# Weight words of the block sums from DRAM, and a scaling behind a maximum on GpSimd

## The chip, the cores and the metric

The kernel runs on 1 core of one Trainium2 chip. The metric is the device time of one execution in microseconds (us). Five engines of the core work beside each other, each through its own instructions in order: PE (TensorE, matrix products), DVE (VectorE), ACT (ScalarE), POOL (GpSimd) and SP (SyncE, which here only issues transfers). An instruction starts when its operands are there and its engine has reached it. Transfers (DMA) run on 16 DMA engines that all queues share.

## The reference

The program is an attention over narrow windows, followed by a feed-forward layer.

```python
B, H, S, D = 8, 8, 576, 64
scores = (q @ k.T) / sqrt(D)                # heads 0-3: the last 32 positions
scores = where(mask, scores, -1e9)          # heads 4-7: every 4th of the last 128
attn = exp(scores - max(scores)); attn = attn / (sum(attn) + 1e-9)
x = (attn @ v).transpose(0, 2, 1, 3).reshape(4608, 512)
h = x @ w_in                                # 512 x 2048, float32
g = h * clip(h + 3, 0, 6) / 6
out = g @ w_out                             # 2048 x 512, float32
```

The weights arrive as 64-bit words. Each float32 operand of the feed-forward products is split into a high and a low part, and three products of parts stand for one product, so the precision of float32 is kept.

## The kernel before, in words

**Weights.** The two weight matrices come in 32 half blocks p of 512 KB (`st`, issued by SP at L484; even p for w_in, odd p for w_out). A half block goes through a chain of seven instructions: ACT takes two scaled copies (U, L499, and Q, L503), DVE shifts (s, L507), sets the sign (j, L513) and adds (a, `cv_add`, L520); what stands in `va` then is the rounded float32 word. ACT copies its high part (h, L523) and DVE subtracts it to get the low part (l, L529), both into the long-lived tiles `wi` or `wo`.

**The first part of the program** (the last addition L520 starts at 151.5 us) is a hand-written order, one string of names, with these seven letters in it for each p. It holds the first attention tiles, all conversions, and the first products of chunk 0 and 1. What comes behind it is a list of operations that a planner sorts: every operation has an engine, an assumed duration, operations it comes after, and slots that it takes and gives back.

**Chunks and groups.** The 4608 tokens make twelve chunks of 384. The first four are plain: first product L545 to L547, gate, second product L595 to L597. The gate's high part `gh` is a CAST on POOL (L560) for these. The other eight chunks go through the products of blocks in seven instead of eight multiplications (L754 to L756 for the first, L745 for the second weight matrix). Their stationary operands are sums and differences of weight blocks. They lie in two DRAM arrays, `sums` and `rights`, and stream back through a ring of eight tiles of 512 KB (L689), issued by SP.

**The block sums** are made once, in the planned part, for 2 sides x 8 pairs k. For each: two DVE additions of high and low part give the words back (`combo_words`, L640), four DVE instructions make the sums (L648), ACT takes the high parts (L652), DVE the low parts (L657), and SP writes both (L675, two transfers of 512 KB). Three plain blocks of each pair are written from `wi` or `wo` (L666, three transfers of 256 KB). The slots of `wi` and `wo` come free when the additions, the plain writes and the products that use them are done.

**Slots.** All these tiles (st, va, wi, wo, v, sh, ring, out) come from one pool of 36 slots of 4 KB a partition. The next user of a slot waits for the last reader of it, whatever engine or queue that is on.

**Attention in the planned part.** A beat of PE computes scores of one tile (L227) and values of an older one (L245). `kq` and `v` (L195, L204) are loaded by SP. Behind the scores DVE takes the largest of each row (L279), multiplies it by minus the scale (L280, 128x6), and ACT takes exponents with it as bias (L288). POOL moves finished attention rows into chunk tiles (L453, L455).

Of the kernel before, what the change touches and what calls it, by code (L numbers as in the profile page):

```python
# [85 lines left out]
def windowed_attention_ffn(ctx: ExitStack, tc: tile.TileContext, qk, vp, w, mask, out, out_t):  # L86
# [183 lines left out]
            in1=mx.rearrange("p (s o) -> p s o", o=1).broadcast_to([P, SLOTS, 2 * QB]), op=ALU.subtract,  # L270
        )

    def scaled_largest(t):
        ps, masked = pss[t]
        if not masked:
            ps = es[t]
        mx = small.tile([P, SLOTS], F32, name="mx")
        pss[t] = ps, mx, masked
        nc.vector.tensor_reduce(out=mx, in_=ps[:, :CH].rearrange("p (s x) -> p s x", x=2 * QB), axis=AX.X, op=ALU.max)  # L279
        nc.vector.tensor_scalar_mul(mx, mx, -SCALE)  # L280

    def exponents(t, j):
        ps, mx, masked = pss[t]
# [233 lines left out]

    def cv_add(p):
        _, _, v, a = parts(p)
        return nc.vector.tensor_tensor(out=v.bitcast(U32), in0=v.bitcast(U32), in1=a.bitcast(U32), op=ALU.add)  # L520

    def cv_high(p):
        ins = nc.scalar.copy(wt(p // 2, p % 2 * 2), parts(p)[2])  # L523
# [3 lines left out]
    def cv_low(p):  # L527
        hi, lo = (wt(p // 2, p % 2 * 2 + i) for i in range(2))
        freed = nc.vector.tensor_tensor(out=lo, in0=parts(p)[2], in1=hi.bitcast(F32), op=ALU.subtract)  # L529
        last["converted"] = freed.ins.name  # L530
        del staged[p]
        converted.add(p)
        return freed

    phs, ts, ghs, gls, po, done = {}, {}, {}, {}, {}, set()

# [95 lines left out]
    ]  # L632
    KEPT = (T1, T3, T4, T2, R11, R21, R22)

    def combo_words(side, k, i, eng):

        if (side, k) not in combos:
            combos[side, k] = w_tile("v", [4, HALF])
        x, v = (win, wout)[side][2 * k + i], combos[side, k]
        eng.tensor_tensor(  # L640
            out=v[:, 2 * i : 2 * i + 2].rearrange("p a n -> p (a n)"), in0=x[:, 0].bitcast(F32), in1=x[:, 1].bitcast(F32), op=ALU.add
        )

    def combo_sum(side, k, i, eng):

# [175 lines left out]
    def attend(bs, pools):  # L821
# [18 lines left out]
            takes=list(room.items()), gives=[("work", len(values))],  # L840
        )
        for ts in scores:
            if by_tensor(ts):
                x = op("DVE", 0.68, lambda ts=ts: scaled_largest(ts), [beat], ahead=EVER)
            else:
                x = op("DVE", 0.55, lambda ts=ts: add_mask(ts), [beat], takes=ONE, gives=[(names[ts], 1)], ahead=EVER)
                released[names[ts]].append(x)
                x = op("DVE", 0.68, lambda ts=ts: scaled_largest(ts), [x], ahead=EVER)
            for i in range(3):
                holds = not i and by_tensor(ts)  # L850
                x = op(
                    "ACT", 0.54, lambda ts=ts, i=i: exponents(ts, i), [x], takes=ONE if holds else (),
                    gives=[(names[ts], 1)] if i == 2 and by_tensor(ts) else (), ahead=EVER,
                )
            if by_tensor(ts):
                released[names[ts]].append(x)
            turned[ts] = turn_over(ts, es, ats, "a", x)
            if ts + NLOAD < T:
                landed_k[ts + NLOAD] = transfer(0.4, 0.82, lambda ts=ts: load_qk(ts + NLOAD), [beat])
# [44 lines left out]

    gated_h = {}

    words, combined, taken = {}, {}, {}

    def combine(side, k):
        x = op("DVE", 0.69, lambda: combo_words(side, k, 0, nc.vector), takes=[("w", 2, SPARE[side][k])], ahead=LEAD_SUMS)  # L910
        words[side, k] = x = op("DVE", 0.69, lambda: combo_words(side, k, 1, nc.vector), [x], ahead=EVER)
        for i in range(4):
            x = op("DVE", 0.42, lambda i=i: combo_sum(side, k, i, nc.vector), [x], ahead=EVER)
        x = op("ACT", 1.05, lambda: combo_high(side, k), [x], ahead=EVER)
# [6 lines left out]
    def last_use(side, f, x):  # L921

        taken[side, f] = x
        if f % 2:
            k = f // 2
            op("NONE", 0.0, lambda: None, [words[side, k], combined[side, k][1], taken[side, f - 1], x], gives=[("w", 2)], ahead=EVER)

    def first(n, after):
        c, f = steps[n]
# [618 lines left out]
```

## Time and profile before

| | us |
|---|---|
| median of 3 runs | 834.25 |
| lowest and highest run | 833.37, 834.36 |
| span of the profiled execution | 832.4 |
| PE busy | 818.8 (98%) |
| DVE busy | 651.2 (78%) |
| ACT busy | 577.0 (69%) |
| POOL busy | 59.3 (7%) |
| moved by DMA | 214.70 MB, mean 258 GB/s |

The profile shows one execution. A run's time contains its span and what lies around it; the median is 1.85 us longer than this span. The chain of waits goes back from the last instruction to what released it each time. The table of windows gives each engine's busy time in stretches of the span, with the share in which the 16 DMA engines were busy and what they moved. In the timeline of SP a row is a transfer's issue, not its movement.

### The profile page before, as it was taken

To read this page: it belongs to the slowest core of one execution; us is meant where nothing else is said; L and a number is where in the kernel's file an instruction comes from. 1 tells how busy PE (TensorE), PEld (TensorE's weight loads), DVE (VectorE), ACT (ScalarE), POOL (GpSimd) and SP (SyncE) were. 2 spreads that over 40 slices of the span, in tenths; PEclk is the share of its full clock that TensorE was granted. 3 is DMA by queue.
4 is the path that set the end of the run, shared out by engine and by line. 5 is a ranking of instruction groups with operands and counts; after the bars stand their busy time and mean duration, and the time that the engine had idled before them with its cause. 6 is when DMAs were issued, how large, how long until landed. Compare 5 with 4: busy or idle time off the path is not lost.

```text
span 832.4 us, 22160 instructions
## 1 busy us (share of the span) xinstructions
PE 818.8 (98%) x8743; PEld 772.0 (93%) x8743; DVE 651.2 (78%) x1325; ACT 577.0 (69%) x1406; POOL 59.3 (7%) x114
## 2 busy tenths in 40 slices
PE   7899999999999999999999999999999999999998
PEld 4788999898898888999999999999999999999998
DVE  4998997656788989888989786888776888445983
ACT  3878775244899884899965699955698845355552
POOL 0000000011223221001300000100001000000000
PEclk9999999999999999999999999999999999999999
DMA  8756433262679999999986798977788777896381
GB/s 289 245 201 239 127 108 118 78 228 93 214 226 304 295 366 357 352 394 393 380 299 228 270 322 312 344 253 258 261 309 308 248 268 254 314 353 239 114 297 57
DMA packets 115783, 214.70 MB, mean 258 GB/s; under 512 B 7520, under 2 KB 40288, under 8 KB 115680
## 3 DMA queue, kind: packets, MB, share of 16 engines
q1 hardware_dynamic: 115680, 213.29, 73.6%
q8 instruction: 69, 1.13, 0.5%
q14 instruction: 34, 0.28, 0.1%
HBM read 174.47 MB, written 38.80 MB: 256 GB/s over the span
## 4 chain that ended last, share of the span: by engine, by line
PE 94%; DVE 2%; DMA 2%; ACT 1%; issue 1%; SPq 0%
PE ps_o L745 28%; PE ps_x L754 10%; PE ps_x L756 9%; PE ps_x L755 9%; PE ps_o L596 5%; PE ps_o L597 5%; PE ps_o L595 5%; PE ps_h L545 5%; PE ps_h L546 5%; PE ps_h L547 5%; PE ps_b L245 2%; PE ps_b L227 1%; PE ps_a L245 1%; PE ps_a L227 1%; DMA st<-in_w 1%; DMA first<-in_v 1%
## 5 line engine op out<-in xcount | busy, mean ns | idle before, releaser
L745 PE MATMUL ps_o<-gh,ring 128*128 128x384 f32 x896 | 230.2, 334 | 0.0
L745 PEld LDWEIGHTS ps_o<-gh,ring 128*128 128x128 f32 x896 | 162.1, 188 | 0.0
L745 PE MATMUL ps_o<-gl,ring 128*128 128x384 f32 x448 | 149.7, 334 | 0.0
L1208 DVE TENSOR_TENSOR gl<-g,gh 128x384 fp32r<-128x384 f32 x224 | 115.8, 552 | 20.8 <-ACT gh L1204 19.8
L1204 ACT CAST gh<-g 128x384 fp32r<-128x384 f32 x224 | 104.7, 512 | 33.3 <-PE ps_o L745 25.1
L754 PE MATMUL ps_x<-x,ring 128*128 128x384 f32 x256 | 88.4, 345 | 0.0
L545 PE MATMUL ps_h<-x,wi 128*128 128x384 f32 x256 | 87.8, 343 | 0.0
L755 PE MATMUL ps_x<-x,ring 128*128 128x384 f32 x256 | 86.1, 336 | 0.0
L756 PE MATMUL ps_x<-x,ring 128*128 128x384 f32 x256 | 86.1, 336 | 0.0
L546 PE MATMUL ps_h<-x,wi 128*128 128x384 f32 x256 | 86.0, 336 | 0.0
L547 PE MATMUL ps_h<-x,wi 128*128 128x384 f32 x256 | 86.0, 336 | 0.0
L745 PEld LDWEIGHTS ps_o<-gl,ring 128*128 128x128 f32 x448 | 84.1, 188 | 0.0
L596 PE MATMUL ps_o<-wo,gh 128*128 128x512 f32 x192 | 74.8, 390 | 0.2 <-DVE wo L529 0.2
L595 PE MATMUL ps_o<-wo,gh 128*128 128x512 f32 x192 | 74.9, 390 | 0.0
L597 PE MATMUL ps_o<-wo,gl 128*128 128x512 f32 x192 | 74.7, 389 | 0.0
L553 ACT ACTIVATE t<-ps_h,three 128x384 f32<-128x384 f32 x64 | 37.0, 581 | 52.4 <-PE ps_h L547 52.1
L756 PE MATMUL ps_x<-cell,ring 128*128 128x384 f32 x192 | 64.9, 338 | 0.0
L754 PE MATMUL ps_x<-cell,ring 128*128 128x384 f32 x192 | 64.7, 337 | 0.0
L755 PE MATMUL ps_x<-cell,ring 128*128 128x384 f32 x192 | 64.7, 337 | 0.0
L1173 DVE TENSOR_TENSOR g<-g 128x768 f32<-128x768 f32 x64 | 60.9, 952 | 0.0
L556 DVE SCALAR_TENSOR_TENSOR t<-t,ps_h 128x384 f32<-128x384 f32 x64 | 35.0, 549 | 23.1 <-ACT t L553 22.7
L392 ACT COPY xf<-xf_t 32x192 f32<-32x192 f32 x144 | 50.4, 350 | 2.8 <-DVE xf L385 0.4
(113 smaller groups left out, 1744.9 us busy)
## 6 DMA issues: line engine op xcount, KB each, us to landing
ring<-sums SPq DMA_DIRECT2D x112, 512.0 KB, 8.3
ring<-rights SPq DMA_DIRECT2D x112, 512.0 KB, 6.7
st<-in_w SPq DMA_DIRECT2D x32, 512.0 KB, 3.9
kq<-in_qk SPq DMA_DIRECT2D x39, 416.0 KB, 5.2
v<-in_v SPq DMA_DIRECT2D x39, 390.0 KB, 6.6
sums<-wi SPq DMA_DIRECT2D x24, 256.0 KB, 6.9
rights<-wo SPq DMA_DIRECT2D x24, 256.0 KB, 6.1
out<-o SPq DMA_DIRECT2D x15, 384.0 KB, 2.8
```

The lines of the kernel that those rows point to most:

```text
L545: nc.tensor.matmul(ph, lhsT=wt(f, 0)[:, ks], rhs=a, start=(kt == 0), stop=False)
L546: nc.tensor.matmul(ph, lhsT=wt(f, 0)[:, ks], rhs=b, start=False, stop=False)
L547: ins = nc.tensor.matmul(ph, lhsT=wt(f, 1)[:, ks], rhs=a, start=False, stop=(kt == NK - 1))
L595: nc.tensor.matmul(po[c][tt], lhsT=gh[:, rows], rhs=wt(f, 2), start=first, stop=False)
L596: nc.tensor.matmul(po[c][tt], lhsT=gh[:, rows], rhs=wt(f, 3), start=False, stop=False)
L597: return nc.tensor.matmul(po[c][tt], lhsT=gl[:, rows], rhs=wt(f, 2), start=False, stop=(f == NF - 1))
L745: nc.tensor.matmul(banks[part][:, :CH], lhsT=right[:, a, cols], rhs=x, start=(start and not i), stop=(i == 2), skip_group_check=True)
L754: nc.tensor.matmul(bank, lhsT=tile_[:, 0, ks], rhs=h[:, kt], start=(start and kt == 0), stop=False, skip_group_check=True)
L755: nc.tensor.matmul(bank, lhsT=tile_[:, 0, ks], rhs=l[:, kt], start=False, stop=False, skip_group_check=True)
L756: nc.tensor.matmul(bank, lhsT=tile_[:, 1, ks], rhs=h[:, kt], start=False, stop=(kt == 1), skip_group_check=True)
L1204: nc.scalar.copy(two[0], gated_tile(g, q, k))
L1208: nc.vector.tensor_tensor(out=two[1], in0=gated_tile(g, q, k), in1=two[0].bitcast(F32), op=ALU.subtract)
```

## The change

Three things change.

1. **A write at conversion.** `cv_add` also issues a transfer on GpSimd's queue that writes the rounded word of the half block (256 KB, 2 KB a partition row) into a new DRAM array `rounded`. There are 32 of them, 8.4 MB. The slot of `va` is now free only when its write has landed.
2. **A load at the block sum.** The 32 DVE additions of `combo_words` go. In their place SP loads the two half blocks of a pair from `rounded` in one transfer of 512 KB (`combo_load`, L645 of the changed kernel; 16 of them, 8.4 MB). The release of the `wi` and `wo` slots no longer names the words. The planner counts the load with 0.5 us of SP and 1.0 us of transfer.
3. **The small multiplication.** Behind the maximum in the planned part, the multiplication of 128x6 by minus the scale goes from DVE to GpSimd (36 of them, L283 of the changed kernel). The planner counts 0.5 us for the maximum and 0.2 us of POOL for the multiplication, where it counted 0.68 us of DVE for both.

```diff
@@ -270,14 +270,17 @@
             in1=mx.rearrange("p (s o) -> p s o", o=1).broadcast_to([P, SLOTS, 2 * QB]), op=ALU.subtract,
         )
 
-    def scaled_largest(t):
+    def plain_largest(t):
         ps, masked = pss[t]
         if not masked:
             ps = es[t]
         mx = small.tile([P, SLOTS], F32, name="mx")
         pss[t] = ps, mx, masked
         nc.vector.tensor_reduce(out=mx, in_=ps[:, :CH].rearrange("p (s x) -> p s x", x=2 * QB), axis=AX.X, op=ALU.max)
-        nc.vector.tensor_scalar_mul(mx, mx, -SCALE)
+
+    def scaled(t):
+        mx = pss[t][1]
+        nc.gpsimd.tensor_scalar_mul(mx, mx, -SCALE)
 
     def exponents(t, j):
         ps, mx, masked = pss[t]
@@ -517,7 +520,9 @@
 
     def cv_add(p):
         _, _, v, a = parts(p)
-        return nc.vector.tensor_tensor(out=v.bitcast(U32), in0=v.bitcast(U32), in1=a.bitcast(U32), op=ALU.add)
+        ins = nc.vector.tensor_tensor(out=v.bitcast(U32), in0=v.bitcast(U32), in1=a.bitcast(U32), op=ALU.add)
+        nc.gpsimd.dma_start(out=rounded[p % 2, p // 4][:, p // 2 % 2], in_=v)
+        return ins
 
     def cv_high(p):
         ins = nc.scalar.copy(wt(p // 2, p % 2 * 2), parts(p)[2])
@@ -531,6 +536,8 @@
         del staged[p]
         converted.add(p)
         return freed
+
+    rounded = tc.dram_tile([2, NF // 2, P, 2, WN], F32, name="rounded")
 
     phs, ts, ghs, gls, po, done = {}, {}, {}, {}, {}, set()
 
@@ -632,14 +639,10 @@
     ]
     KEPT = (T1, T3, T4, T2, R11, R21, R22)
 
-    def combo_words(side, k, i, eng):
-
-        if (side, k) not in combos:
-            combos[side, k] = w_tile("v", [4, HALF])
-        x, v = (win, wout)[side][2 * k + i], combos[side, k]
-        eng.tensor_tensor(
-            out=v[:, 2 * i : 2 * i + 2].rearrange("p a n -> p (a n)"), in0=x[:, 0].bitcast(F32), in1=x[:, 1].bitcast(F32), op=ALU.add
-        )
+    def combo_load(side, k):
+
+        combos[side, k] = v = w_tile("v", [4, HALF])
+        nc.sync.dma_start(out=v.rearrange("p a n -> p (a n)"), in_=rounded[side, k].rearrange("p i n -> p (i n)"))
 
     def combo_sum(side, k, i, eng):
 
@@ -840,12 +843,12 @@
             takes=list(room.items()), gives=[("work", len(values))],
         )
         for ts in scores:
-            if by_tensor(ts):
-                x = op("DVE", 0.68, lambda ts=ts: scaled_largest(ts), [beat], ahead=EVER)
-            else:
+            x = beat
+            if not by_tensor(ts):
                 x = op("DVE", 0.55, lambda ts=ts: add_mask(ts), [beat], takes=ONE, gives=[(names[ts], 1)], ahead=EVER)
                 released[names[ts]].append(x)
-                x = op("DVE", 0.68, lambda ts=ts: scaled_largest(ts), [x], ahead=EVER)
+            x = op("DVE", 0.5, lambda ts=ts: plain_largest(ts), [x], ahead=EVER)
+            x = op("POOL", 0.2, lambda ts=ts: scaled(ts), [x], ahead=EVER)
             for i in range(3):
                 holds = not i and by_tensor(ts)
                 x = op(
@@ -904,11 +907,10 @@
 
     gated_h = {}
 
-    words, combined, taken = {}, {}, {}
+    combined, taken = {}, {}
 
     def combine(side, k):
-        x = op("DVE", 0.69, lambda: combo_words(side, k, 0, nc.vector), takes=[("w", 2, SPARE[side][k])], ahead=LEAD_SUMS)
-        words[side, k] = x = op("DVE", 0.69, lambda: combo_words(side, k, 1, nc.vector), [x], ahead=EVER)
+        x = transfer(0.5, 1.0, lambda: combo_load(side, k), takes=[("w", 2, SPARE[side][k])], ahead=LEAD_SUMS)
         for i in range(4):
             x = op("DVE", 0.42, lambda i=i: combo_sum(side, k, i, nc.vector), [x], ahead=EVER)
         x = op("ACT", 1.05, lambda: combo_high(side, k), [x], ahead=EVER)
@@ -923,7 +925,7 @@
         taken[side, f] = x
         if f % 2:
             k = f // 2
-            op("NONE", 0.0, lambda: None, [words[side, k], combined[side, k][1], taken[side, f - 1], x], gives=[("w", 2)], ahead=EVER)
+            op("NONE", 0.0, lambda: None, [combined[side, k][1], taken[side, f - 1], x], gives=[("w", 2)], ahead=EVER)
 
     def first(n, after):
         c, f = steps[n]
```

The order of PE's instructions is the same in both kernels. Since the planner sorts again, the others move.

**SP, where the ring begins.** `rights` and `sums` are the DRAM arrays, `wo` the converted weights, `sh` and `v` the block sums' parts, and `v<-rounded` the new load. Before:

```order
L675 DMA sums_107<-sh_4463 128x4x256
L675 DMA sums_107<-v_4129 128x4x256
L666 DMA rights_108<-wo_1895 256x1x256
L666 DMA rights_108<-wo_1963 256x1x256 x2
L689 DMA ring_4672<-sums_107 128x2x512
L666 DMA rights_108<-wo_2065 256x1x256
L666 DMA rights_108<-wo_2160 256x1x256 x2
L666 DMA rights_108<-wo_1522 256x1x256
L666 DMA rights_108<-wo_1502 256x1x256 x2
L689 DMA ring_4734<-sums_107 128x2x512
L689 DMA ring_4773<-sums_107 128x2x512
L689 DMA ring_4820<-sums_107 128x2x512
```

Changed:

```order
L645 DMA v_4664<-rounded_107 128x1024
L645 DMA v_4669<-rounded_107 128x1024
L645 DMA v_4677<-rounded_107 128x1024
L669 DMA rights_109<-wo_1919 256x1x256
L669 DMA rights_109<-wo_1990 256x1x256 x2
L669 DMA rights_109<-wo_2095 256x1x256
L669 DMA rights_109<-wo_2191 256x1x256 x2
L678 DMA sums_108<-sh_4633 128x4x256
L678 DMA sums_108<-v_4056 128x4x256
L669 DMA rights_109<-wo_1535 256x1x256
L669 DMA rights_109<-wo_1515 256x1x256 x2
L692 DMA ring_4787<-sums_108 128x2x512
```

Before, the first ring load stood ahead of six plain writes; now all plain writes and all 16 loads of words, three of them in this piece, stand ahead of it.

**SP, behind the first ring loads**, up to the second pair of attention loads. Before:

```order
L689 DMA ring_4910<-sums_107 128x2x512
L675 DMA rights_108<-sh_4888 128x4x256
L675 DMA rights_108<-v_4402 128x4x256
L195 DMA kq_5015<-in_qk 128x832
L204 DMA v_5017<-in_v 128x780
L675 DMA rights_108<-sh_4906 128x4x256
L675 DMA rights_108<-v_4428 128x4x256
L689 DMA ring_5041<-sums_107 128x2x512
L903 DMA out_0<-o_5043 128x512
L689 DMA ring_5075<-sums_107 128x2x512
L903 DMA out_0<-o_5043 128x512
L903 DMA out_0<-o_5092 128x512
```

Changed:

```order
L692 DMA ring_4902<-sums_108 128x2x512
L678 DMA rights_109<-sh_4647 128x4x256
L678 DMA rights_109<-v_4167 128x4x256
L678 DMA rights_109<-sh_4881 128x4x256
L678 DMA rights_109<-v_4413 128x4x256
L692 DMA ring_4927<-sums_108 128x2x512
L678 DMA rights_109<-sh_4945 128x4x256
L678 DMA rights_109<-v_4471 128x4x256
L678 DMA rights_109<-sh_4949 128x4x256
L678 DMA rights_109<-v_4664 128x4x256
L195 DMA kq_5056<-in_qk 128x832
L204 DMA v_5061<-in_v 128x780
```

Of the block sums' writes to `rights`, one pair stood ahead of the attention loads kq and v here, and now four do.

**POOL, in the same stretch.** Before, where `gh` is the last gate of the plain chunks and `raw` are attention rows:

```order
L560 CAST gh_4945<-t_4924 128x384
L455 COPY raw_5756<-xf_5722 128x2x192
L455 COPY raw_5756<-xf_5808 128x2x192
L455 COPY raw_5999<-xf_5827 128x2x192
L455 COPY raw_5999<-xf_5894 128x2x192
L455 COPY raw_6150<-xf_5924 128x192
```

Changed, with the multiplication of `mx`:

```order
L567 CAST gh_4988<-t_4965 128x384
L283 TENSOR_SCALAR mx_5076<-mx_5076 128x6
L283 TENSOR_SCALAR mx_5254<-mx_5254 128x6
L283 TENSOR_SCALAR mx_5417<-mx_5417 128x6
L283 TENSOR_SCALAR mx_5583<-mx_5583 128x6
L458 COPY raw_5596<-xf_5119 128x2x192
L458 COPY raw_5596<-xf_5132 128x2x192
L283 TENSOR_SCALAR mx_5715<-mx_5715 128x6
L458 COPY raw_5863<-xf_5601 128x2x192
L283 TENSOR_SCALAR mx_5910<-mx_5910 128x6
L458 COPY raw_5863<-xf_5740 128x2x192
```

The multiplications now stand between the gates and the copies in POOL's order; the last two shown are behind the first copy into a newly taken `raw` slot.

## The prediction

> **What bounds the kernel now.** I read the page first, then what PE waits for, then the windows. PE is the bound:
>
> ```profile
> span 832.4 us, 22160 instructions
> PE 818.8 (98%) x8743; PEld 772.0 (93%) x8743; DVE 651.2 (78%) x1325; ACT 577.0 (69%) x1406; POOL 59.3 (7%) x114
> PE 94%; DVE 2%; DMA 2%; ACT 1%; issue 1%; SPq 0%
> ```
>
> PE waits for little. The list of its waits shows for what (total, times, longest):
>
> ```profile
> PE ps_a L227 <- issue: 2.7, 2, 2.1
> PE ps_a L354 <- DVE x L315: 2.4, 3, 0.8
> PE ps_a L354 <- ACT e L291: 1.8, 2, 0.9
> PE ps_a L237 <- DMA first<-in_v: 0.8, 1, 0.8
> PE ps_o L596 <- DVE wo L529: 0.2, 1, 0.2
> ```
>
> These are five of its seven rows; the rest is smaller. The windows of 50 us show where they can lie (PE, PEld, DVE, ACT, POOL busy, granted clock, DMA share, GB/s):
>
> ```profile
> 0.00:50.00 50.00, 40.35 (x1108) 30.38 (x1109) 36.67 (x89) 31.89 (x71) 0.59 (x6) 0.97 0.80 270
> 50.00:100.00 50.00, 49.33 (x408) 44.27 (x408) 46.90 (x98) 38.90 (x79) 0.00 (x0) 1.00 0.53 176
> 100.00:150.00 50.00, 50.00 (x256) 45.66 (x255) 41.30 (x79) 33.74 (x62) 0.00 (x0) 1.00 0.44 134
> 300.00:350.00 50.00, 50.00 (x507) 45.83 (x509) 44.03 (x88) 34.00 (x91) 7.02 (x8) 1.00 1.01 352
> 350.00:400.00 50.00, 50.00 (x774) 48.13 (x757) 43.87 (x105) 46.91 (x121) 5.24 (x13) 1.00 1.06 393
> ```
>
> Two things are to be seen. Behind 100 us PE is never idle, so work taken from DVE there buys nothing: the change can save only what lies in the first 70 us, where it leaves DVE's order as it was. And between 300 and 400 us the DMA engines are full (share 1.01 and 1.06) with PE just still covered. Whatever adds bytes there draws on that cover.
>
> **The change part by part. Removed.** 32 additions of about 0.7 us and 36 multiplications on DVE:
>
> ```profile
> L640 DVE TENSOR_TENSOR v<-wi 128x512 f32<-128x512 f32 x16 | 10.8, 697 | 0.0
> L640 DVE TENSOR_TENSOR v<-wo 128x512 f32<-128x512 f32 x16 | 10.8, 702 | 0.0
> L280 DVE TENSOR_SCALAR mx<-mx 128x6 f32<-128x6 f32 x36 | 8.2, 227 | 1.2
> ```
>
> That is 29.8 us off DVE, all behind 155 us, where PE waits for nothing. Value: 0. The cover is PE's own work. A gain would need PE gaps that DVE causes there, and there are none, so below zero is excluded except for noise.
>
> **The writes at conversion** cost nothing to DVE. They cost DMA time in the startup, where PE hangs on single loads. The chain of waits there (start, length, what):
>
> ```profile
> 38.45 6.41 DMA first<-in_v
> 44.99 0.21 PE ps_a L237
> 56.99 7.13 DMA st<-in_w
> 67.53 0.50 PE ps_o L596
> ```
>
> Two loads are on the chain, and the DMA engines were nearly full while they moved. Below the windows stand three of the additions behind which the writes go out, and the median landing of an `st` load:
>
> ```profile
> 38.00:40.00 2.00, 2.00 (x56) 1.58 (x57) 1.97 (x4) 2.00 (x5) 0.00 (x0) 1.00 0.83 322
> 42.00:44.00 2.00, 2.00 (x14) 1.74 (x12) 2.00 (x6) 2.00 (x5) 0.00 (x0) 1.00 1.02 386
> 44.00:46.00 2.00, 1.20 (x83) 1.01 (x85) 1.48 (x3) 2.00 (x7) 0.00 (x0) 1.00 1.03 414
> 62.00:64.00 2.00, 2.00 (x13) 2.00 (x12) 1.35 (x4) 1.17 (x3) 0.00 (x0) 1.00 1.00 397
> 37.31 0.68 DVE L520 CUSTOM_DVE_ANT_0 va<-va 128x1024 uint16<-128x1024 uint16 x1
> 39.45 0.68 DVE L520 CUSTOM_DVE_ANT_0 va<-va 128x1024 uint16<-128x1024 uint16 x1
> 60.09 0.70 DVE L520 CUSTOM_DVE_ANT_0 va<-va 128x1024 uint16<-128x1024 uint16 x1
> st<-in_w SPq DMA_DIRECT2D x32, 512.0 KB, 3.9
> ```
>
> One addition ends at 37.99 and one at 40.13; both writes move while the load `first` is on its way, from its issue at 38.45 to its landing at 44.86. A write of 256 KB (0.262 MB) takes 0.65 us at 400 GB/s, so the two shift the landing by 0 to 1.3 us. A third write, at 60.79, stands beside the `st` load that is under way from 56.99 to 64.12: 0 to 0.65 us. Behind 64 us there is room (share 0.44 to 0.53). Some of the 1.95 us will be absorbed where a transfer's order is luckier. I take +1.5, range 0 to 2.
>
> The slots of `va` come free later too. No row gives how far each slot's next user is. I take it that a write which lands within the 3.9 us of an `st` load, twice its size, is hidden, and put this at 0; the dearer case is a rival.
>
> [...]
>
> **The loads at the block sums.** By the order shown, 10 of the 16 loads stand behind the attention loads that went out at 252.80 us. Ten loads of 0.524 MB are 5.24 MB, 13.3 us at 393 GB/s. What room is there?
>
> ```profile
> 250.00:270.00 20.00, 20.00 (x462) 17.37 (x461) 17.37 (x42) 18.10 (x52) 6.07 (x12) 1.00 0.92 305
> 270.00:283.00 13.00, 13.00 (x158) 11.49 (x156) 11.50 (x28) 11.47 (x40) 2.07 (x5) 1.00 0.98 334
> 283.00:290.00 7.00, 7.00 (x132) 6.38 (x128) 6.86 (x20) 6.72 (x24) 2.84 (x7) 1.00 0.75 206
> 290.00:300.00 10.00, 10.00 (x230) 8.58 (x230) 9.13 (x19) 8.84 (x25) 1.91 (x3) 1.00 1.08 377
> ```
>
> With 1.06 as full, the free DMA time is 2.3 us from 252.8 to 270, then 1.0, 2.0 and 0, and 2.3 in the window from 300 to 350 shown above (share 1.01): 7.6 us. So 13.3 - 7.6 = 5.7 us are carried into the ring's stretch. There the writes of block sums to `rights` come earlier in the order: four more transfers of 512 KB ahead of the second pair of attention loads, 5.3 us. Together 11.0 us late, less the 1.5 us by which PE is late itself: 9.5 us. These are the loads' margins:
>
> ```profile
> 341.88 0.34 SPq L195 DMA_DIRECT2D kq<-in_qk  x1
> 342.27 0.69 SPq L204 DMA_DIRECT2D v<-in_v  x1
> DMA to landing us min/median/max: 8.0/8.0/8.0
> L227 PE MATMUL ps_b<-kq x48: 216/216/240, 357.9 to 358.9; 64*32 64x64 f32 x48
> ```
>
> `v` lands 8.0 us behind 342.27, at 350.3, and PE uses it at 358: margin 7.7. So PE waits 9.5 - 7.7 = 1.8 us there. At 352 GB/s, what the stretch from 300 moved, the same sum is 14.9 + 6.0 - 7.6 - 1.5 - 7.7 = 4.1 us. The low end is 0: if the planner's earlier start of the sums moves loads into the emptier stretch before 250 us. Later the lateness shrinks, since the writes that came earlier are missing later.
>
> **The multiplication on POOL** is in the middle of a chain. Before, POOL waited for slots in the same place, and nothing stood behind it:
>
> ```profile
> 374.69 0.51 POOL L455 COPY raw<-xf 128x384 f32<-128x384 f32 x1 [44.16 <-DMA ring<-sums]
> 380.39 0.17 DVE L280 TENSOR_SCALAR mx<-mx 128x6 f32<-128x6 f32 x1
> 381.50 0.57 ACT L288 ACTIVATE e<-e,mx 128x64 f32<-128x64 f32 x2
> ```
>
> POOL waited 44 us for a transfer to free a slot. In the changed order a multiplication stands behind such a copy. The copy began 5.7 us ahead of the multiplication's old place, and ACT's exponents 1.1 us behind it. If transfers are 7 us late, ACT stands still for a microsecond or two, and its gates wait with it. Elsewhere the hop adds a start on another engine, covered by that 1.1 us. I put this at 0 to 2, and take +0.7.
>
> So the stretch from 320 to 400 costs 1.8 + 0.7 = 2.5 us, range 0 to 6. The sum is 832.4 + 1.5 + 2.5 = 836.4. The median of the runs was 1.85 above the profiled span, so **838.2 us**.
>
> **The rivals.**
>
> *All of it is hidden* (not slower). The writes miss the two loads, being spread over 16 engines in an order that favours SP's queue, and the planner's early loads use the emptier time. For it: the ring's eight tiles, and the margin of 7.7 us. Against it: the shares of 1.01 and 1.06 from 300 to 400 us. It gives 834.3 to 835.7.
>
> *The full DMA stretch breaks down.* Ring tiles come late as well as attention loads, the copies on POOL hold the multiplication, and ACT in its order holds the gates. For it: the share of 1.06, where nothing can be caught up until 400 us. Price: with the margin used up before the second pair of loads, by ring tiles that were late, 4 to 9 of the 9.5 us remain; with the startup 839.8 to 844.8. It decides once ring tiles land later than their use, for which 7.7 us of lateness stand.
>
> *Slow writes.* GpSimd's transfers take longer than the 6.4 us that `first` took in the full stretch, and the slots of `va` come free late for SP's `st` loads and ACT's first copies between 60 and 160 us. PE has already waited 0.2 us for a converted `wo` (the first list), so nothing is left there, and writes of 8 to 10 us would cost 2 to 4 us beside the forecast: 840 to 842. For it: POOL's queue has carried no such transfer before. Against it: the DMA share of 0.44 to 0.53 there. [...]
>
> *Faster.* The mechanism would be DVE's 29.8 us and the earlier release of `wi` and `wo`, which lets the ring start sooner. It needs PE gaps behind 100 us, and there are none; only the gaps of the startup (9.65 us in the first window) could shrink, and the order there is unchanged. Price: at most 2 us, so 832.3.
>
> **How the numbers follow.** About 0.2% (1.7 us) is what a measurement of this kernel can tell from no change, so the lines are at 832.6 and 835.9. Forecast 0.45, breaking down 0.22, slow writes 0.08, all hidden 0.21, faster 0.04. The forecast's own range is 836 to 840.5, so it counts as slower; so do the next two: 0.75. All hidden is the same: 0.21. For eight in ten I leave out the faster end and the far end of the break-down: 834.4 to 843.5.
>
> **What would show it.** Right: in the changed profile the load `first` lands up to 1.3 us later and the wait of L237 for it grows; the list of PE's waits has rows for `ring`, `kq` or `v` between 320 and 400 us, and the DMA share is near 1.06 from 270 us on. The POOL step is right if exponents wait for `mx` of POOL there. Wrong: PE is at 50.00 of 50 in the window of 300 to 400 (then the second term is 0), or L237's wait is unchanged (then the first is), or new waits stand between 80 and 160 us (slow writes), or the rows from `rounded` come so early that the share before 250 us takes them.

## The result, and the profile after

The changed kernel takes 845.96 us (median of four runs, 844.12 to 848.60), the kernel before 834.25 us. The ratio is 1.0146 (1.0126 to 1.0166): slower by 11.7 us. The prediction was 838.2 us with a range of 834.4 to 843.5, so the sign was right and the size was not; the time lies above the range. The profiled execution is the longest of the four, so a second profile (e14, span 844.5 us) stands beside it.

The head of the page, the shares of the chain that ended last, the row of GpSimd's queue, and the two new kinds of transfer with their median time from issue to landing:

```profile
span 846.8 us, 22256 instructions
PE 826.0 (98%) x8743; PEld 777.2 (92%) x8743; DVE 623.8 (74%) x1257; ACT 577.5 (68%) x1406; POOL 83.9 (10%) x182
q0 software_dynamic: 2560, 8.39, 2.6%
PE 83%; DMA 10%; DVE 4%; SPq 1%; ACT 1%; issue 1%; POOL 0%; POOLq 0%
rounded<-va POOLq DMA_DIRECT2D x32, 256.0 KB, 4.0
v<-rounded SPq DMA_DIRECT2D x16, 512.0 KB, 7.7
```

The change did what it says: DVE has 68 instructions and 27.4 us less, GpSimd's queue moved 8.39 MB, and 16 loads of words came in. But DMA's share of the chain went from 2% to 10%. PE's list of waits (total, times, longest) says where:

```profile
PE ps_x L757 <- DMA ring<-sums: 5.4, 2, 3.7
PE ps_a L237 <- DMA first<-in_v: 2.2, 1, 2.2
PE ps_b L245 <- DMA v<-in_v: 1.8, 2, 1.1
```

The row of `first` was 0.8 before; the other two were not there. The windows of 50 us place them (PE, PEld, DVE, ACT, POOL busy, granted clock, DMA share, GB/s):

```profile
0.00:50.00 50.00, 41.02 (x1055) 30.94 (x1059) 33.35 (x79) 29.32 (x65) 2.94 (x10) 0.95 0.82 282
300.00:350.00 50.00, 46.26 (x496) 40.88 (x495) 40.41 (x78) 32.00 (x80) 9.84 (x13) 0.97 1.06 381
350.00:400.00 50.00, 46.41 (x796) 43.57 (x795) 35.02 (x81) 43.41 (x118) 3.19 (x9) 1.00 1.06 392
```

PE is idle for 7.3 us between 300 and 400, where it was idle for nothing, with the DMA share at 1.06. The granted clock is below 1.00 in two of these windows, which no sum of waits contains.

**The largest wait** is the one for the ring's first tile. SP's timeline of the changed kernel (start, length, what; a row is an issue) up to that tile, with the two writes to `sums` at 324.34 and 325.63 left out:

```profile
315.49 1.56 SPq L645 DMA_DIRECT2D v<-rounded  x3
317.71 5.84 SPq L669 DMA_DIRECT2D rights<-wo  x6
326.28 4.10 SPq L669 DMA_DIRECT2D rights<-wo  x3
330.43 5.13 SPq L692 DMA_DIRECT2D ring<-sums  x7
```

And the same place before:

```profile
309.91 0.82 SPq L689 DMA_DIRECT2D ring<-sums  x1
310.78 6.28 SPq L666 DMA_DIRECT2D rights<-wo  x6
317.10 5.41 SPq L689 DMA_DIRECT2D ring<-sums  x7
```

The first tile's load went out at 330.43 instead of 309.91, 20.5 us later, since all plain writes and all loads of words now stand ahead of it. PE's use of the tile before (its timeline), and the chain after:

```profile
328.83 0.34 PE L754 MATMUL ps_x<-cell,ring 128*128 128x384 f32 x1
```

```profile
330.43 6.63 DMA ring<-sums
337.19 0.41 PE ps_x L757
```

Before, that load had 18.9 us from its issue to its use. After, it landed at 337.06. PE had come 4.46 us late into this stretch, so it was ready for the tile at 328.83 + 4.46 = 333.3, and 337.06 - 333.3 gives the 3.7 us of the list.

**Then PE ran at half rate.** Windows of 2 us behind that wait, in the changed kernel:

```profile
335.00:337.00 2.00, 0.00 (x0) 0.00 (x0) 1.60 (x3) 0.00 (x0) 1.10 (x1) 1.00 1.03 378
337.00:339.00 2.00, 1.81 (x8) 1.75 (x9) 0.06 (x1) 0.42 (x2) 0.00 (x0) 0.81 1.05 407
339.00:341.00 2.00, 2.00 (x6) 1.54 (x6) 1.18 (x2) 0.79 (x2) 0.00 (x0) 0.50 1.12 364
341.00:343.00 2.00, 2.00 (x99) 1.52 (x98) 0.11 (x1) 0.00 (x0) 0.00 (x0) 0.83 0.93 319
```

The granted clock fell to 0.50 and was back after some 3.5 us. The nine matmuls of the output block behind the wait took 3.72 us from the first's start to what follows them, and 2.16 us before.

Three more waits follow until 382 us: `v` 1.1 us, a later ring tile 1.7 us, `v` 0.7 us. With 3.7 and the 1.65 that the half rate cost (PE stood 10.01 us behind its old times after the block, 8.36 ahead of it) they make 8.9 of the 9.8 us that this stretch lost. PE's order is the same in both kernels, so such shifts can be read matmul by matmul; a table of them stands in the next section.

### The profile page after: what moved, and what is told of

Its sections match the earlier page's. It is cut to its first block, busy times and chain, and to the rows that moved or that the text cites. A ratio compares the mean times of both kernels' runs of the same rounds, so it can differ in the third digit from the quotient of the medians.

```text
span 846.8 us, 22256 instructions
## 1 busy us (share of the span) xinstructions
PE 826.0 (98%) x8743; PEld 777.2 (92%) x8743; DVE 623.8 (74%) x1257; ACT 577.5 (68%) x1406; POOL 83.9 (10%) x182
## 3 DMA queue, kind: packets, MB, share of 16 engines
q0 software_dynamic: 2560, 8.39, 2.6%
## 4 chain that ended last, share of the span: by engine, by line
PE 83%; DMA 10%; DVE 4%; SPq 1%; ACT 1%; issue 1%; POOL 0%; POOLq 0%
PE ps_o L748 28%; PE ps_x L757 9%; PE ps_x L759 9%; PE ps_x L758 9%; PE ps_o L602 4%; PE ps_o L603 4%; PE ps_o L604 4%; PE ps_h L552 4%; PE ps_h L554 3%; PE ps_h L553 3%; DMA rights<-wo 3%; DMA v<-in_v 3%; PE ps_b L245 2%; PE ps_b L227 1%; PE ps_a L227 1%; DMA sums<-wi 1%
## 5 line engine op out<-in xcount | busy, mean ns | idle before, releaser
L1060 DVE TENSOR_TENSOR s<-ps_x,s 128x384 f32<-128x384 f32 x64 | 35.3, 552 | 26.6 <-ACT s L1053 22.2
L395 ACT COPY a<-a_t 32x192 f32<-32x192 f32 x144 | 50.4, 350 | 2.9 <-DVE a L388 0.5
```

## The experiments

Two theories were set against each other. **Order:** the ring's first tile is late because of what stands ahead of it in SP's queue, and bytes alone cost little. **Bytes:** 16.8 MB more are too much for a DMA that is full. Beside them the startup's writes and the multiplication on GpSimd were each tried alone. The medians of the kernel before in the four comparisons were 833.92 to 834.45 us, and each run is held against its own. The ratios, with 95% intervals, are those on record, and differ from the quotient of the medians by up to 0.11%, about 0.9 us.

This table is worked out from the PE timelines: by how many us a matmul starts later in one profile of a kernel than in the profile of before. The columns are places, by their time before: ahead of the load `first`, behind it, end of the startup, the ring's first tile, behind the output block, behind the second pair of attention loads, end. The last column is the difference of the medians.

| kernel | 34 | 47 | 70 | 329 | 332 | 368 | end | timed |
|---|---|---|---|---|---|---|---|---|
| changed | 2.5 | 4.4 | 4.3 | 8.4 | 10.0 | 14.3 | 14.4 | +11.7 |
| changed again (e14) | -0.5 | 2.0 | 1.6 | 6.6 | 8.2 | 12.0 | 12.1 | +13.8 |
| e1 writes only | 0.6 | 2.1 | 2.3 | 2.3 | 2.3 | 2.3 | 2.3 | +3.6 |
| e2 loads, no writes | 0.2 | 0.9 | -0.1 | 4.7 | 7.5 | 8.9 | 8.9 | +8.6 |
| e3 half loads | 0.1 | 2.8 | 3.5 | 3.6 | 3.6 | 6.5 | 6.5 | +7.0 |
| e4 multiplication on DVE | 2.1 | 3.3 | 2.8 | 3.3 | 3.3 | 9.9 | 9.9 | +12.2 |
| e7 eight loads | -0.1 | 2.0 | 1.7 | 2.8 | 2.8 | 2.8 | 4.6 | +4.6 |
| e8 bytes, old order | 1.8 | 1.6 | 1.4 | 1.3 | 1.3 | 1.3 | 2.2 | +1.6 |
| e9 plain writes earlier | 0.3 | 1.5 | 1.0 | 1.1 | 1.1 | 1.1 | 1.1 | +3.1 |

**The writes alone (e1).** The kernel before with the 32 writes added, and nothing else:

```diff
+        nc.gpsimd.dma_start(out=rounded[p % 2, p // 4][:, p // 2 % 2], in_=v)
```

> The kernel before with the 32 writes of the rounded words added, and nothing else: the additions for the block sums stay on DVE, nothing is loaded back, the small multiplication stays on DVE. Theory (the writes collide with single loads of the startup): PE's shift of the changed kernel up to 70 us, 4.3 us in its profile, is the writes' doing to 2 us or more; time 836 to 838.5, PE never idle behind 100 us. Rival (the startup's shift is an accident of that one profile, since 2.5 us of it were there before the first write at 22 us): within 0.7 us of before, 833.6 to 835.

Measured: 838.01 us, ratio 1.0047 (1.0035 to 1.0059), +3.6. No new wait stands behind 70 us. In the startup PE's wait ahead of L237 has grown from 0.8, and the clock follows:

```profile
PE ps_a L237 <- ACT t L557: 2.3, 1, 2.3
44.00:46.00 2.00, 0.48 (x3) 0.09 (x1) 1.77 (x4) 2.00 (x7) 0.00 (x0) 1.00 1.05 427
46.00:48.00 2.00, 1.23 (x94) 1.25 (x96) 0.00 (x0) 0.74 (x3) 0.00 (x0) 1.00 1.02 407
48.00:50.00 2.00, 2.00 (x20) 1.83 (x11) 1.63 (x5) 0.82 (x2) 0.00 (x0) 0.50 0.64 249
50.00:52.00 2.00, 2.00 (x10) 2.00 (x8) 1.93 (x6) 1.20 (x3) 0.00 (x0) 0.65 0.01 5
```

ACT is named as the releaser, but the engine that is full there is the DMA (1.05 and 1.02). The 3.6 us are the startup's part. The writes landed in 3.6 us (median) and DVE's addition kept its length: its mean in ns was 685 before, and in e1 (both from 18 to 150 us) it is 684:

```profile
L520 DVE CUSTOM_DVE_ANT_0 va<-va 128x1024 uint16<-128x1024 uint16 x31 | 20.8, 684 | 0.1
```

**Which writes (e5, e11).** e5 leaves out the first eight writes, e11 only the third and the fourth, the two that move beside `first`:

```diff
+        if len(converted) >= 8:                # e5
+        if len(rounded_by) not in (3, 4):      # e11
+            nc.gpsimd.dma_start(out=rounded[p % 2, p // 4][:, p // 2 % 2], in_=v)
```

> As the kernel with the writes alone, but without the first eight of the 32 (those up to about 70 us); 24 stay. Theory (the writes cost only where they move beside single loads that PE hangs on, in the first 70 us, and the wait then leaves PE at a slow pace for some us): 834 to 835.3, no shift of PE. Rival (slots of va that come free late, or the writes between 70 and 160 us, take part in it): 836 or more, with a shift of PE between 70 and 160 us.

> As the kernel with the writes alone, without its third and fourth write, those that move beside the load first between 38 and 45 us; 30 stay. Theory of the prediction (these two carry two thirds of the startup's cost by shifting that load): 834.3 to 836. Rival (every write of the first 70 us shifts something that is on PE's way; these two are no more than their share, a quarter of the eight): 836.5 to 838.5.

Measured: e5 833.81 us, 0.9988 (0.9976 to 1.0000); e11 834.21 us, 1.0011 (0.9997 to 1.0024). Neither can be told from before, and in e11 the wait is gone:

```profile
PE ps_a L237 <- DMA first<-in_v: 0.2, 1, 0.2
```

So the two writes carry the startup's cost, and the other 30 show none: in e11's profile PE's shift is -0.1 us from 70 us to the end, and the upper end of its interval is 2.0 us.

**The queue or the bytes (e6).** All 32 writes issued by ACT instead of GpSimd:

```diff
     def cv_high(p):
         ins = nc.scalar.copy(wt(p // 2, p % 2 * 2), parts(p)[2])
...
+        nc.scalar.dma_start(out=rounded[p % 2, p // 4][:, p // 2 % 2], in_=parts(p)[2])
```

> As the kernel with the writes alone (all 32), but issued on ACT's queue behind the copy of the high part instead of on GpSimd's. Theory (the bytes in the full DMA engines are what costs): 836.5 to 838.5, as with GpSimd's queue (838.0). Rival (it is GpSimd's queue: slow starts of its transfers, or DVE and GpSimd in each other's way): at most 835.5.

Measured: 836.74 us, 1.0032 (1.0019 to 1.0045), +2.5. Most of the cost stays on another queue, which speaks for the bytes; the intervals of e1 and e6 overlap, so the 1.1 us between them are not shown to be the queue's. Its one profile does not settle where the cost lies: `first` took 7.2 us there and PE waited 1.1 us for it, but PE was 2.0 us late already at 34 us.

**The loads alone (e2).** The changed kernel without its writes; the loads read the attention input in its place, so the block sums, and with them the output, are not the reference's:

```diff
-        nc.gpsimd.dma_start(out=rounded[p % 2, p // 4][:, p // 2 % 2], in_=v)
-        nc.sync.dma_start(out=v.rearrange("p a n -> p (a n)"), in_=rounded[side, k].rearrange("p i n -> p (i n)"))
+        nc.sync.dma_start(out=v.rearrange("p (i a) n -> p i (a n)", i=2), in_=qk[2 * k : 2 * k + 2].rearrange("t h d x -> (h d) t x")[:, :, :WN])
```

> The changed kernel without the 32 writes; the 16 loads of 512 KB read the attention's input instead (wrong sums, same bytes, 2 KB a piece in place of 4 KB), so the order of the planned part is that of the changed kernel. Theory (the loads and their order fill the DMA engines between 250 and 400 us): the shift that PE collects between 320 and 370 us stays at 8 to 10.5 us, only the startup's part goes: 842.5 to 844.5. Rival (the writes' late landing and their slots push the whole planned part into the full stretch): the shift there falls below 5 us, 836 to 840.

Measured: 843.04 us, 1.0102 (1.0089 to 1.0115), +8.6. With e1's 3.6 that is 12.2, against 11.7 for both. Its longest wait and a window behind it:

```profile
PE ps_x L754 <- DMA ring<-sums: 4.6, 2, 4.2
333.00:335.00 2.00, 1.50 (x5) 1.54 (x6) 0.01 (x1) 0.00 (x0) 0.00 (x0) 0.50 1.04 392
```

The same wait and the same half rate, without any write.

**Half the bytes (e3).** The loads move 256 KB, and the sums are made from the first half block of each pair, so that part of the output is not the reference's:

```diff
+        nc.sync.dma_start(out=v[:, 0:2].rearrange("p a n -> p (a n)"), in_=rounded[side, k][:, 0])
```

> The changed kernel with loads of half the size: 256 KB instead of 512 KB, and the block sums made from the first half (wrong sums). Order and count of all instructions stay. Theory (bytes): the ten loads behind 252 us take 6.5 us less, so the first ring tile is no longer 3.7 us late, the slow PE behind that wait goes with it, and the waits for v get smaller: PE's shift between 320 and 370 us falls from 9.7 to between 1 and 4.5 us, time 837 to 841. Rival (order: the plain writes and the block sums' writes now stand ahead of the ring and of the attention loads, whatever the loads weigh): shift still 7 us or more, time 843 to 846.

Measured: 841.46 us, 1.0084 (1.0069 to 1.0099), +7.0. The ring's first tile is in time, and what is left are short waits later:

```profile
PE ps_b L245 <- DMA v<-in_v: 1.7, 2, 1.0
PE ps_x L757 <- DMA ring<-sums: 0.6, 1, 0.6
```

By the table the stretch costs 2.9 us instead of 9.8. The writes are all there, so e1's 3.6 us are in the time too, and 3.6 + 2.9 = 6.5 of the 7.0 us are placed. The order of the instructions is that of the changed kernel here, and half of the loads' bytes already have the first tile in time. So the bytes count too, and this run's rival, the same loss whatever the loads weigh, is out; the time lies 0.5 us above the theory's range.

**Half of the loads (e7).** The block sums of `w_out` are made by DVE's additions as before, those of `w_in` by loads; all 32 writes stay:

```diff
+LOADED = frozenset((0, k) for k in range(8))
-        x = transfer(0.5, 1.0, lambda: combo_load(side, k), takes=[("w", 2, SPARE[side][k])], ahead=LEAD_SUMS)
+        if (side, k) in LOADED:
+            words[side, k] = x = transfer(0.5, 1.0, lambda: combo_load(side, k), takes=[("w", 2, SPARE[side][k])], ahead=LEAD_SUMS)
+        else:
...
```

> The changed kernel with the eight block sums of w_out made by the DVE additions of before, those of w_in by loads; all 32 writes stay, the multiplication stays on GpSimd. Four loads are left behind 252 us (2.1 MB, 5.3 us), less than the 7.6 us of room, and the first ring load stands ahead of the last plain writes again. Theory (the late loads for w_out and the order that they bring fill the stretch): the shift between 320 and 370 us is under 1.5 us, only the startup's 3.6 us is left: 837 to 839. Rival (the full stretch is lost with any loads at all, or by the multiplication on GpSimd): shift 4 us or more there, 841 to 846.

Measured: 838.82 us, 1.0053 (1.0034 to 1.0073), +4.6. The ring's stretch costs nothing. Beside the startup's part about 1 us appears between 258 and 300 us of before, with a wait of 0.8 us for DVE, and about a microsecond and a half at 402 us, where one matmul waits for ACT:

```profile
PE ps_o L758 <- ACT gh L1220: 0.8, 1, 0.8
```

**All the bytes on the old order (e8).** The kernel before with 16 transfers of 512 KB from DRAM to DRAM in SP's queue, at the places of the first additions:

```diff
+            nc.sync.dma_start(out=scrap[side, k], in_=qk[2 * k : 2 * k + 2].rearrange("t h d x -> (h d) t x")[:, :, :WN])
```

> The kernel before, with 16 transfers of 512 KB from DRAM to DRAM put into SP's queue where the block sums' first additions stand; nothing waits for them, and the rest of the order is that of before. Theory (bytes and order both count; in the old order the ring and the attention loads stand ahead, and the later transfers come behind the ring's first loads): PE is late by 0 to 4 us between 320 and 400 us, 834.3 to 838.5. Rival (bytes alone: 8.4 MB in the full stretch cost what the change costs there): 841 to 845.

Measured: 835.86 us, 1.0010 (0.9995 to 1.0024), not to be told from before. The DMA is as full as in the changed kernel, and PE is covered but for 0.7 us behind 350 us:

```profile
300.00:350.00 50.00, 50.00 (x529) 45.99 (x526) 44.11 (x90) 34.63 (x93) 7.86 (x9) 1.00 1.06 380
PE ps_b L245 <- DMA v<-in_v: 0.7, 1, 0.7
```

This is the run that parts the theories: 381 and 380 GB/s at a share of 1.06 in both, 3.74 us of PE lost in this window there and nothing here. So a full DMA alone did not make PE wait there.

**The order alone (e9).** The changed kernel with one number altered, which lets the planner start the plain writes up to 150 us ahead of their due time instead of 90:

```diff
-EARLY = 90.0
+EARLY = 150.0
```

> The changed kernel with one number of the planner changed: the plain writes of weight blocks (three of 256 KB for each pair) may start 150 instead of 90 us ahead of their due time. All 32 writes, all 16 loads and the multiplication on GpSimd stay. Theory (not the 8.4 MB as such, but what stands ahead of the ring's first tiles and of the attention loads between 280 and 350 us costs the 8.6 us): with the plain writes gone to the emptier DMA engines before 250 us PE waits for nothing there, and only the startup's 3.6 us is left: 837 to 839. Rival (any 8.4 MB more between 140 and 320 us end up in the full stretch): 841 or more.

Measured: 837.02 us, 1.0048 (1.0030 to 1.0066), +3.1. The plain writes of `wo` by their line, first of the changed kernel, then of e9 (shortest, median and longest issue in ns, first and last start), with e9's window:

```profile
L669 SPq DMA_DIRECT2D rights<-wo x24: 513/652/1353, 295.5 to 329.1; - x24
```

```profile
L669 SPq DMA_DIRECT2D rights<-wo x24: 525/682/1696, 226.7 to 254.0; - x24
300.00:350.00 50.00, 50.00 (x530) 45.94 (x518) 44.45 (x86) 38.02 (x94) 8.67 (x13) 1.00 0.96 331
```

With every byte kept, and the plain writes some 70 us earlier, PE waits for nothing behind 70 us. What is left fits the cost of e1's writes. The ring's first load went out at 303.73, with one load of words and no plain write of `wo` behind it. The DMA had room for the plain writes where they went: its share from 200 to 250 us is 0.88 here and 0.67 in the changed kernel, and from 300 to 350 us it fell from 1.06 to 0.96. So the loss comes from the new bytes and the order together: the bytes on the old order (e8), the bytes with the plain writes moved out of the way (e9) and half of the loads' bytes on the new order (e3) each leave the ring's first tile in time.

**The multiplication (e4, e12).** e4 is the changed kernel with it back on DVE; e12 is the kernel before with it moved to GpSimd and nothing else:

```diff
-        nc.gpsimd.tensor_scalar_mul(mx, mx, -SCALE)
+        nc.vector.tensor_scalar_mul(mx, mx, -SCALE)
```

> The changed kernel with the small multiplication back on DVE (0.18 us of DVE in the planner's table). Theory (the hop over POOL does not matter, DMA does): 844 to 846.5. Rival (copies on POOL that wait for slots hold the multiplication, ACT stands in front of the exponents and holds the gates): 2 us or more faster than the changed kernel, 841 to 844.

> The kernel before with the small multiplication on GpSimd alone: no writes, no loads, additions on DVE. Theory (the hop is covered and DVE's time is not on the path): 833.5 to 835, no wait of PE behind 70 us. Rival (the hop delays exponents, ACT stands, gates come late): 835.5 or more.

Measured: e4 846.69 us, 1.0142 (1.0126 to 1.0158), the same as the changed kernel; e12 833.85 us, 1.0005 (0.9991 to 1.0018), the same as before. No cost and no gain of the multiplication shows in either. e12's interval reaches from -0.8 to +1.5 us, so a few tenths are not excluded by the times; in its profile PE's shift is 1.7 us at 70 us and the same at the end, so PE lost nothing in the planned part. e4 is the weaker test, since the planner sorted once more and the waits came elsewhere:

```profile
PE ps_b L245 <- DMA v<-in_v: 3.2, 2, 2.5
PE ps_x L757 <- DMA ring<-sums: 1.6, 2, 1.2
```

The total came out alike, but mostly through an attention load instead of the ring's first tile.

**Both causes removed (e10, e13).** Both have `EARLY` at 150. In e10 the block sums k = 0 and 1 of both sides go back to DVE's additions and their eight writes are left out (12 loads, 24 writes). In e13 only `w_in`'s k = 1 does, whose writes are the third and the fourth (15 loads, 30 writes):

```diff
+LOADED = frozenset((s, k) for s in range(2) for k in range(2, 8))              # e10
+LOADED = frozenset((s, k) for s in range(2) for k in range(8)) - {(0, 1)}      # e13
...
+        if (p % 2, p // 4) in LOADED:
+            nc.gpsimd.dma_start(out=rounded[p % 2, p // 4][:, p // 2 % 2], in_=v)
...
```

> As the kernel with earlier plain writes, and the four block sums of k = 0 and 1 made by DVE's additions, so that the eight half blocks p below 8, the ones converted first, are not written: 24 writes, 12 loads. Theory (startup writes and order are the whole cost): 833.3 to 835.3, the time of before, no wait of PE behind 70 us. Rival (something of the change costs beside these two): 836 or more. A gain over before would need PE gaps that the change closes; none is expected.

> The two causes taken away together: the plain writes may start 150 us ahead, and the block sum of w_in with k = 1 is made by DVE's additions, so that its two half blocks, whose writes move beside the load first, are not written; 30 writes and 15 loads stay, the multiplication stays on GpSimd. Theory (the two writes in the startup and the order in front of the ring are the whole of the 11.7 us): 833.3 to 835.3, no wait of PE behind 70 us. Rival (something is left over, as the run with twelve loads, 5.5 us above before, may mean): 836.5 or more.

Measured: e10 839.47 us, 1.0071 (1.0053 to 1.0088), +5.5, a miss; e13 835.47 us, 1.0018 (1.0006 to 1.0031), +1.5. In e10 a new wait appeared near 258 us of before, for DVE, to which the additions had come back at another place in its order; its startup also shows the clock at half, ahead of its first write:

```profile
PE ps_h L554 <- DVE t L565: 1.7, 1, 1.7
32.00:34.00 2.00, 2.00 (x88) 1.60 (x93) 1.44 (x3) 1.81 (x5) 0.00 (x0) 0.50 0.50 98
```

The shift grows by 3.1 us, from 2.1 at 70 us to 5.2 at 320, and this wait is the largest single piece of it. The rest of the median, some 2.4 us, is not settled: whether its unprofiled runs met the half clock in the startup more often than those of before is not known. e13 closes 10.2 of the 11.7 us. Its 1.5 us lie just above the expected range, and its interval, from 1.0006 on, excludes equality, so a small rest stays unexplained. Its profile is one of its shorter runs (834.57 us); PE ends 0.3 us later there than before, and the one wait behind 70 us is 0.5 us long (at 304 us, for ACT).

**The changed kernel again (e14).**

> The changed kernel as it is, once more, since its first profile fell on the slowest of its runs (848.6 against a median of 845.96). Theory: time 844 to 847.5; the startup's shift in this profile between 1.5 and 4 us, the shift between 320 and 370 us 8.5 to 10.5 us, with PE at a slow pace behind its longest wait there. Rival (the first profile was untypical in the full stretch too): a shift there outside 7 to 11 us, or no slow pace.

Measured: 847.73 us, 1.0168 (1.0146 to 1.0189), 0.2 us above the expected time; the shift between 320 and 370 us was 9.1. The second profile has the same three waits:

```profile
PE ps_x L757 <- DMA ring<-sums: 5.4, 3, 3.5
PE ps_a L237 <- DMA first<-in_v: 2.5, 1, 2.5
PE ps_b L245 <- DMA v<-in_v: 1.3, 2, 0.7
```

None of these kernels is shown to be faster than before. PE has no idle time behind 70 us there, so e13's 15 loads could at best be free.

## Why the prediction was right and wrong

**DVE's 29.8 us are worth nothing: right.** DVE's busy time fell by 27.4 us and no profile shows PE or the end gaining from it.

**The writes: the place was right, the size was not.** The term was that two writes shift the landing of `first` by 0 to 1.3 us and a third one an `st` load by up to 0.65: +1.5, range 0 to 2. e11 confirms the two writes, and e5 shows no cost of the later ones; e1 measured 3.6 us. In the changed kernel's chain the load took 8.19 us where it had taken 6.41:

```profile
40.23 8.19 DMA first<-in_v
```

That is 1.8 us longer, above the 1.3 that two writes make at the rate of the sum; L237's wait grew by 1.5 us in e1. What the sum lacked altogether is what PE did after a wait of some two microseconds: in e1 and in the changed kernel its clock was at 0.50 for 3.4 us. A wait was priced at its own length, and it can cost more: 1.65 us more behind the ring's first tile. How much of the 3.6 us each part makes in the timed runs was not separated; e1's profile is the shortest of its runs.

**Slow writes: rejected.** The writes landed in 4.0 us (median), DVE's addition took 684 ns beside them in e1 against 685, and no wait came up between 80 and 160 us. Only the two writes beside `first` took longer than the 6.4 us that the rival named, 7.8 and 6.8 us.

**The loads: the mechanism was right, and the place where the margin was taken was wrong.** This is the step that failed. The prediction summed 13.3 us of loads and 5.3 us of earlier writes, took off the free time, and held the 9.5 us of lateness against the margin of the second pair of attention loads (7.7 us), which left 1.8. But those loads are not the first to be used behind the new bytes. The ring's first tile is, and the order that stands ahead of the prediction shows it moved behind every plain write and every load of words. Its load had 18.9 us from issue to use, and the profile of before has the landings of the first twelve such loads (shortest, median, longest):

```profile
DMA to landing us min/median/max: 6.6/8.3/9.7
```

So its margin was 9.2 to 12.3 us. In front of it, behind the attention loads of 252.80, came ten loads of words (5.24 MB), six plain writes (1.57 MB) and one more pair of block sums (1.05 MB). These are 7.86 MB, or 20.0 us at the 393 GB/s of the prediction; less the 5.3 us that were free until 300 us, 14.7 us; measured, the stretch from those attention loads to the ring's first issue was 16.2 us longer. The 1.5 us by which PE itself was held to be late do not come off, as they did in the prediction: those attention loads went out at 257.09, 4.3 us later, when PE was 4.3 us late. e2 bears this out, where PE was 0.3 us late at 320 us and the wait was the longest, 4.2 us. So the same working at the right place gives a wait of 2.4 to 5.5 us (an estimate made afterwards, with nothing taken off for room after 300 us), where 3.7 were measured, and the half rate comes on top. At the second pair of attention loads, where the prediction looked, PE did not wait in the changed kernel: by then it was 11 us late, and its `v` landed at 368.42, ahead of the use at 369.15. e9 shows that what stands ahead of the ring was the cause: the same bytes with the plain writes ahead cost nothing in the stretch. e8 shows the other half: the bytes on the old order are covered.

**After that, lateness did not shrink.** The prediction said that it would, since writes that came earlier are missing later. With a share of 1.06 until 400 us there was no room, and three more waits (1.1, 1.7, 0.7) followed, the first of them at the first attention loads behind the ring. The half rate behind the ring's first tile cost 1.65 us. The term of 2.5 us, with a range of 0 to 6, measured 9.8 in the profile and 8.6 in e2.

**The rival "the full DMA stretch breaks down" was the nearest.** Its condition, ring tiles that land later than their use, is what happened, and its price of 4 to 9 us for the stretch was nearly right. It got a chance of 0.22 where the order already spoke for it, and its end of 844.8 was cut off by the range. With 3.6 for the startup in place of 1.5, its upper end would have been near 847.

**The multiplication: +0.7 is not borne out.** Neither e4 nor e12 shows a cost, and e12's profile shows no wait for it; its timed interval (-0.8 to +1.5 us) alone would not exclude 0.7. The chain on POOL that was described decided nothing here.

A detail of the change was told wrongly above: the second number of the planner's entry for a load, 1.0, is a size (512 KB), which the planner counts as 1.3 us, and not a time in us.

## What to carry to other kernels

When a change adds transfers to a queue that is full, find the first transfer behind them in the new order that something waits for, and take the margin there, as use less issue less landing; a margin further down says nothing. The same bytes cost nothing that could be told with the old order ahead of the ring (e8), and nothing in the full stretch once other writes had left before it (e9); 8.6 of the 11.7 us came back with one number of the planner. Price a new wait of PE of about two microseconds or more with the half-rate time that can follow it, and look at the granted clock behind it: in the changed kernel waits of 2.2 and 3.7 us were followed by 3.4 us at 0.50, and in e9 one of 2.1 us by 1.00.

## What the hardware showed that was not expected

**The clock fell after waits of about 2 us, and not always.** Around `first` PE's idle time of 2.2 to 2.5 us was followed by a clock of 0.50 in the changed kernel, e1 and e14. In e9 a wait of 2.1 us was followed by 1.00. Two windows of 3.41 us of the changed kernel, then the wait and two such windows of e9:

```profile
44.72:48.13 3.41, 1.66 (x11) 1.21 (x9) 2.96 (x6) 3.41 (x10) 0.00 (x0) 1.00 1.03 408
48.13:51.54 3.41, 2.99 (x100) 2.85 (x101) 0.88 (x3) 0.58 (x3) 0.00 (x0) 0.50 0.88 349
```

```profile
PE ps_a L237 <- DMA first<-in_v: 2.1, 1, 2.1
45.21:48.62 3.41, 2.04 (x101) 1.98 (x102) 1.36 (x4) 2.12 (x8) 0.00 (x0) 1.00 1.02 408
48.62:52.03 3.41, 3.41 (x108) 2.83 (x107) 3.34 (x10) 3.03 (x6) 0.31 (x1) 1.00 0.11 41
```

In the changed kernel the clock is at 0.50 from 24.23, from 48.13 and from 338.26 us, for 3.41 us each time. PE was not idle throughout ahead of it: in the 3.41 us that end at these points it was idle for 1.82, 1.75 and 2.34 us. In e9 PE was idle for the 2.1 us of its wait, 1.37 of them in the first of its two windows, and the clock stayed at 1.00. What parts the two cases is not shown.

**It is also part of why profiles of one startup differ.** Here is the window from 28 to 36 us of before, and of e12, whose transfers are the same:

```profile
28.00:36.00 8.00, 6.44 (x214) 5.54 (x215) 7.69 (x23) 5.50 (x13) 0.00 (x0) 1.00 0.71 232
```

```profile
28.00:36.00 8.00, 6.21 (x196) 4.51 (x199) 6.69 (x18) 5.27 (x14) 0.00 (x0) 0.72 0.73 261
```

At 34 us e12 is 3.8 us behind the profile of before, and 1.7 at its end, though the medians are the same. Single profiles of this kernel are therefore good for places, and medians for sizes of 1 to 3 us.

**SP's issues of one kind differ in length.** In the changed kernel three plain writes took 4.10 us to issue at 326.28, 1.37 us each, where the median issue of that line is 0.65. The ring's first load followed at 330.43, right behind the end of the last of them at 330.38, so this too delayed it. What lengthens an issue is not shown: in e9, where these writes went out at 226.7 to 254.0 us, the median was 0.68 and the longest 1.70.
